# Linear-attention numerators: two feature groups in two 64-column halves of TensorE, in plain fp32 instead of split fp32r

## The chip, the cores and the metric

The kernel runs on one core of a Trainium2 chip. A core has a matrix engine (TensorE, PE in the profile; its weight loads are PEld), a vector engine (VectorE, DVE), an engine for functions and copies (ScalarE, ACT), a general one (GpSimd, POOL) and one that here only issues transfers (SyncE, SP). The metric is device time in microseconds (us), lower is better. Three runs of the kernel before took 760.90, 761.03 and 761.24 us; the median is 761.03.

## The reference

For 2048 rows x of 640 features, the output is a gated sum g * a + (1 - g) * b, with g the sigmoid of a row's product with a vector. b is a feed-forward block (640 to 1728 with SiLU, and back). a is linear attention with 32 heads of 20 features; the changed part lies in its last lines:

```
phi_q = concatenate([softmax(pq), softmax(-pq)])        # 40 features a head
kv  = einsum("bhsf,bhsd->bhfd", phi_k, v)               # 40 x 20 a head
num = einsum("bhqf,bhfd->bhqd", phi_q, kv)              # the numerators
den = einsum("bhqf,bhf->bhq", phi_q, z) + 1e-6
a   = (num / den) @ wo
```

The kernel divides by the denominators, and multiplies by g, in the features of q before the numerators are formed, so that the numerators go straight on to the product with wo.

## The kernel before, in words

TensorE multiplies a stationary operand (at most 128 rows by 128 columns, loaded as weights) with a moving one. The kernel reaches fp32 accuracy with the reduced type fp32r by splitting each operand into a high part and the remainder: the high part is a copy by ACT, the remainder a subtraction by DVE or POOL (`split`), and a product is three matmuls, high by high, high by low and low by high (`PASSES`). Three places use plain fp32 matmuls instead: the products of small weights (lines 231 and 317) and the transposes with an identity (lines 898, 946 and 991).

The work goes in stages: keys and values and their sums per head (the last of their projections, L470, starts at 172 us), the feed-forward block in four blocks of 512 rows (L518 and L706), and then the queries, in 8 pieces of 256 rows. In the last stage the projections of later pieces (L429), their softmax features (on DVE, ACT and POOL) and the transposes, numerators and output products of earlier pieces take turns.

For one piece u the steps are these:

- `t_mm(u, i)` transposes the features with PE (L991). The 32 heads have 1280 feature columns. They are taken in groups of 120 columns, three heads each; a pair i (0 to 4) holds two such groups, and i = 5 holds the last 80 columns, two heads. The result, up to 120 partitions by 2 x 256, is in PSUM.
- `t_hi` copies it to SBUF as the high part (ACT, L1002), `t_lo` makes the low part (DVE, L1008).
- `n_mm(u, gp, a)` forms the numerators of pair i = 2 gp + a: 120 features by 256 rows against `kvw`, whose blocks are 120 columns wide. The first group of a pair fills the first 60 columns of its block and zeros stand in the other 60; the second group the other way about. So the six matmuls of a pair (two groups, three passes) add up in the same 120 partitions of PSUM (L1128). The rest has three matmuls.
- `n_hi`, `n_lo` split the numerators into high and low (L1142, L1144, L1150) for the next product.
- `w_mm` multiplies them with `wo` (L1171), with 120 partitions a pair, and the result is added to the feed-forward part and stored.

`make_kvw` (L886) prepares `kvw` and `kvwr` (for the rest) once: transposes of the sums per head, a split into high and low, zeros by POOL. `wo_load` and `wo_split` bring in `wo` in five chunks of 120 rows.

The order is written out by hand. Inside the last stage `inorder(PE, DVE, ACT, POOL)` fixes the order of each of these engines to that of the code in `step(u)` for u = 1 to 5 and `last_steps` after them; all loads and stores are on SP's queue. A middle step contains, on PE, the numerators of pairs 4 and 5 of the piece before, then for piece u pairs 0, 1, 2 and 3, each followed by other work, with projections and output products between.

Of the kernel before, what the change touches and what calls it, by code (L numbers as in the profile page):

```python
# [16 lines left out]
P = 128  # L17
S = 2048
D = 640
# [9 lines left out]
FR = F - NF * P  # L29
GR = 6  # L30
GW = GR * DH
NG = H // GR
REST = D - NG * GW
NJ = 2 * NG + 1
# [26 lines left out]
def mix_kernel(ctx: ExitStack, tc: tile.TileContext, xT, wqT, wkc, wkr, wv, bd, bdc, cst, wo, w1, w1r, w2, out):  # L61
# [665 lines left out]

    def wo_load(c):
        wor_raw[c] = r = raw(f"wo{c}")
        nc.sync.dma_start(r[:GW, :D], wo[c * GW : (c + 1) * GW, :])  # L730

    def wo_split(c):
        r = wor_raw.pop(c)
        split(WO[:GW, c, 0, :D], WO[:GW, c, 1, :D], r[:GW, :D])

    def stack(dst, src, hi, col, n=GW):

# [148 lines left out]

    def make_kvw():

        parts = [w.rearrange("p j f -> p (j f)").rearrange("p (i q f) -> p i q f", q=4, f=KD) for w in kvw]
# [12 lines left out]
        for j0, n, pt in pts:  # L902
            n = min(n, 2 * NG - j0)
            i0, i1 = j0 // 2, (j0 + n) // 2
# [12 lines left out]

    es = {}

# [72 lines left out]
                    pT[:w, jj * 256 + k * P : jj * 256 + (k + 1) * P], es[2 * PB[u] + k][:, j * GW : j * GW + w], ident  # L992
                )

    def t_hi(u, i):
        pT = fTs[u, i]
        nj, w = (2, GW) if i < NG else (1, RC)
        if (u, i) < (0, 4):
            f = slot(f"fT{u}_{i}")
        else:  # L1000
            f = slot(f"fT{u}_{i}", fu, "u", 3) if i % 2 == 0 else slot(f"fT{u}_{i}", tb, "fT", 2)
        nc.scalar.copy(f[:w, 0, : nj * 256], pT[:w, : nj * 256])  # L1002
        fTs[u, i] = f, pT

    def t_lo(u, i):
        f, pT = fTs[u, i]
        nj, w = (2, GW) if i < NG else (1, RC)
        nc.vector.tensor_tensor(  # L1008
            f[:w, 1, : nj * 256], pT[:w, : nj * 256], f[:w, 0, : nj * 256].bitcast(F32), op=ALU.subtract
        )  # L1010
        fTs[u, i] = f

    for n in range(2):
# [2 lines left out]
    with inorder(PE, DVE, ACT, POOL):  # L1016
        last_dense(2)
        last_dense(3)
        load_gates(NB - 1)
        load_fused(0)  # L1020
        last_dense(4)
        WQ = big("wq")
        zbc = wslot("zbc")
        nc.sync.dma_start(zbc, kv_d[KF].partition_broadcast(P))

        def fuse(gi):
            return fused(kvb["bd"], WQ[:, :, 0, :], WQ[:, :, 1, :], gi)
# [23 lines left out]
        kvw = [wslot(f"kvw{h}", F32R)[:GW, : 2 * NG * GW].rearrange("p (j f) -> p j f", f=GW) for h in range(2)]  # L1051
        kvwr = fu.tile([RC, 2, GW], F32R, name="kvwr")
# [36 lines left out]
        acc_mm(1)  # L1089
        acc_out(1)  # L1090
        acc_mm(2)
        acc_out(2)
        for i in range(4):
            t_mm(0, i, bank)
            t_hi(0, i)
            t_lo(0, i)
# [15 lines left out]
    WOR = tb.tile([GW, D], F32R, name="wor_s")  # L1112
    wor = raw("wor")
    for k in range(3):
        nc.sync.dma_start(wor[k * REST : (k + 1) * REST, :D], wo[NG * GW :, :])

    def n_mm(u, gp, a):
        if (gp, a) == (0, 0):
            oTs[u] = tb.tile([GW, 2, NG + 1, 256], F32R, tag="oT", name=f"oT{u}", bufs=2)
        if a == 0:  # L1120
            pns[u, gp] = single(f"pn{u}_{gp}").rearrange("p (a s) -> p a s", a=2)
        i = 2 * gp + a
        nj, w = (2, GW) if i < NG else (1, RC)
        f = fTs.pop((u, i))
        n = 0
        for jj in range(nj):
            for hk, hp in PASSES:
                nc.tensor.matmul(  # L1128
                    pns[u, gp][:GW, a, :],
                    kvw_of(hk, 2 * i + jj)[:w],  # L1130
                    f[:w, hp, jj * 256 : (jj + 1) * 256],
                    start=(n == 0),
                    stop=(n == 3 * nj - 1),
                )
                n += 1

    pns = {}

    def n_hi(u, gp):
        o, pn = oTs[u], pns[u, gp]  # L1140
        if gp < 2:
            nc.scalar.copy(o[:, 0, 2 * gp : 2 * gp + 2, :], pn[:GW])  # L1142
        else:
            nc.scalar.copy(o[:, 0, 4, :], pn[:GW, 0])  # L1144
            nc.scalar.activation(o[:, 1, 5, :], pn[:GW, 1], AF.Copy, scale=stk[:GW, 0:1])

    def n_lo(u, gp):
        o, pn = oTs[u], pns.pop((u, gp))
        k = slice(2 * gp, 2 * gp + 2) if gp < 2 else slice(4, 5)
        nc.vector.tensor_tensor(o[:, 1, k, :], pn[:GW, : k.stop - k.start], o[:, 0, k, :].bitcast(F32), op=ALU.subtract)  # L1150
        if gp == 2:
            nc.vector.scalar_tensor_tensor(
                o[:, 0, 5, :], pn[:GW, 1], stk[:GW, 1:2], o[:, 1, 5, :].bitcast(F32), op0=ALU.mult, op1=ALU.add
            )

    ws = {}
# [1 line left out]
    def w_mm(u, m0, n):  # L1158
# [9 lines left out]
        for a in range(n):  # L1168
            ds = slice((m0 + a) * P, (m0 + a + 1) * P)
            for k, (c, ho, hw) in enumerate(todo):  # L1170
                nc.tensor.matmul(  # L1171
                    pa[:, a, :],
                    WO[:GW, c, hw, ds] if c < NG else WOR[:, ds],
                    o[:, ho, c, :],
                    start=(k == 0),
                    stop=(k == len(todo) - 1),
                )
# [49 lines left out]
    def t_pair(u, i):  # L1227
        for k in (i, i + 1):
            t_mm(u, k)
        for k in (i, i + 1):  # L1230
            t_hi(u, k)

    def n_first(u):
        n_mm(u, 0, 0)
        t_mm(u, 2)
        t_hi(u, 2)
        n_mm(u, 0, 1)
        t_mm(u, 3)
        n_hi(u, 0)
        t_hi(u, 3)  # L1240

    def n_second(u):
        n_mm(u, 1, 0)
# [2 lines left out]
        n_mm(u, 1, 1)  # L1246

    def second_out(u):
        t_hi(u, 4)
        t_hi(u, 5)  # L1250
        n_hi(u, 1)
        t_lo(u, 4)
        t_lo(u, 5)
        n_lo(u, 1)

    def step(u):
# [3 lines left out]
        n_lo(u - 1, 2)  # L1260
        if u == 1:
            on(a, lambda t: q_sub(t, 1), q_exp)
        t_lo(u, 0)
        t_lo(u, 1)
        if u == 1:
            on(a, q_norm, q_sum)
            x_next(2)
# [2 lines left out]
        if u > 1:  # L1270
            on(a, q_small)
        n_first(u)
        t_lo(u, 2)
        if u > 1:
            on(b, q_max)
        n_lo(u, 0)
        t_lo(u, 3)
        if u == 1:
            on(a, q_small)
            on(b, q_max)  # L1280
# [29 lines left out]
    def last_steps(u):  # L1310
# [4 lines left out]
        t_pair(u, 0)  # L1315
        on(a, q_norm_sum)
        on(b, q_max)
        t_lo(u, 0)
        on(b, lambda t: q_sub(t, 0))
        t_lo(u, 1)  # L1320
        w_mm(u - 1, 0, 2)
        on(b, lambda t: q_sub(t, 1))
        w_out(u - 1, 0)
# [8 lines left out]
            t_mm(u, i)  # L1332
        n_hi(u, 0)
        for i in (2, 3):
            t_hi(u, i)
        t_lo(u, 2)
        n_lo(u, 0)
        t_lo(u, 3)
        on(b, q_norm_sum, q_small, q_mul)
        w_mm(u - 1, 2, 2)  # L1340
        n_second(u)
# [5 lines left out]
            for i in range(2):  # L1347
                t_mm(v, i, ks=(k,))
        w_copy(u - 1, 4)
        t_hi(v, 0)  # L1350
        n_mm(u, 2, 0)
        n_mm(u, 2, 1)
        t_lo(v, 0)
        t_hi(v, 1)
        t_lo(v, 1)
        w_add(u - 1, 4)
        n_hi(u, 2)
        n_lo(u, 2)
        n_first(v)
        t_lo(v, 2)  # L1360
        n_lo(v, 0)
        t_lo(v, 3)
        w_mm(u, 0, 2)
        n_second(v)
        w_out(u, 0)
# [11 lines left out]
    with inorder(PE, DVE, ACT, POOL):  # L1377
# [4 lines left out]
            n_lo(0, gp)  # L1382
        for i in (4, 5):
            t_mm(0, i)
            t_hi(0, i)
            t_lo(0, i)
# [72 lines left out]
```

## Time and profile before

| | before |
|---|---|
| median of 3 runs | 761.03 us |
| span of the profiled execution | 759.8 us |
| PE busy | 755.0 us |
| DVE busy | 371.6 us |
| ACT busy | 266.4 us |
| POOL busy | 264.3 us |
| first and last start of the numerators' matmuls | 578.6 and 744.9 us |

The profiled execution's own time is known by its span, from its first to its last instruction. A group row of the profile gives line, engine and operation, then what is written and read, the shape, the count, the busy time in us and the mean length of one in ns. For a matmul, 120*120 120x256 means a stationary operand of 120 rows and 120 columns and a moving one of 120 rows and 256 columns. The length of one matmul includes its way through the array, which overlaps with the next matmul, so the price of one in a run of equal ones is the distance of their starts. A row of the timeline gives the start in us, the length in us and how many like instructions in a row it stands for. Times in square brackets, or after the second bar, are idle time of the engine before the instruction and what ended it.

### The profile page before, as it was taken

The numbers are of one execution on the slowest core, as the hardware profiler recorded it, in microseconds if no ns is written. First come the engines' busy times: TensorE is split into PE (matmuls) and PEld (weight loads), VectorE is DVE, ScalarE is ACT, GpSimd is POOL, SyncE is SP. The second block draws the span as 40 slices with busy tenths as digits, with TensorE's granted clock in tenths as the row PEclk, the third lists the DMA queues.
The fourth block names the chain that finished last, engine by engine and source line by source line (L and its number), as shares of the span: only waits on it lengthen the run. The fifth ranks groups of instructions, "written<-read, shape, count | busy, mean of one in ns | idle before, by whom it ended". The sixth has DMA issues, their size and how long they took to land.

```text
span 759.8 us, 10642 instructions
## 1 busy us (share of the span) xinstructions
PE 755.0 (99%) x4249; PEld 664.9 (88%) x4249; DVE 371.6 (49%) x664; ACT 266.4 (35%) x483; POOL 264.3 (35%) x165
## 2 busy tenths in 40 slices
PE   9999999999999999999999999999999999999998
PEld 8888888888888888888888888888999999999998
DVE  4676666676641221112211122134578888787861
ACT  5444444337541311122111222224354443334341
POOL 2388777768000000000000000000356766855551
PEclk9999999999999999999999999999999999999999
DMA  7111111112650220002200014022003332111222
GB/s 254 54 53 53 53 53 53 60 49 83 206 175 1 69 83 1 1 0 72 84 0 1 1 40 154 8 81 85 6 29 127 97 104 70 54 52 43 70 70 91
DMA packets 35259, 50.17 MB, mean 66 GB/s; under 512 B 3541, under 2 KB 22885, under 8 KB 35210
## 3 DMA queue, kind: packets, MB, share of 16 engines
q1 hardware_dynamic: 35210, 49.50, 20.7%
q8 instruction: 33, 0.54, 0.3%
q14 instruction: 16, 0.13, 0.1%
HBM read 38.37 MB, written 11.11 MB: 65 GB/s over the span
## 4 chain that ended last, share of the span: by engine, by line
PE 97%; DVE 1%; DMA 0%; POOL 0%; ACT 0%; issue 0%; SPq 0%; POOLq 0%; DVEq 0%; ACTq 0%
PE acc L706 25%; PE ph L518 23%; PE kvp L470 16%; PE pq L429 9%; PE pa L1171 9%; PE pn L1128 4%; PE kv L440 2%; PE pT L991 2%; PE kvp L535 2%; PE kvp L328 1%; PE kvq L328 1%; PE pwk L317 1%; PE pwq L231 1%; DMA wvr<-wv 0%; POOL eq L840 0%; PE kvp L451 0%
## 5 line engine op out<-in xcount | busy, mean ns | idle before, releaser
L120 DVE TENSOR_TENSOR u<-ph,u 128x512 fp32r<-128x512 f32 x48 | 33.2, 692 | 188.5 <-ACT u L118 188.5
L706 PE MATMUL acc<-u,w 128*128 128x512 f32 x480 | 114.2, 391 | 0.0
L891 POOL MEMSET kvw<- 120x600 f32 x2 | 1.2, 598 | 321.1 <-PE ph L518 321.1
L706 PEld LDWEIGHTS acc<-u,w 128*128 128x128 f32 x480 | 89.7, 188 | 19.2
L518 PE MATMUL ph<-xf,w 128*128 128x512 f32 x420 | 99.7, 390 | 0.0
L521 ACT ACTIVATE ph<-ph 128x512 f32<-128x512 f32 x48 | 27.9, 582 | 192.6 <-PE ph L518 192.6
L518 PEld LDWEIGHTS ph<-xf,w 128*128 128x128 f32 x420 | 78.7, 188 | 16.6
L470 PE MATMUL kvp<-wh,xa 128*128 128x500 f32 (+1 forms) x420 | 93.0, 357 | 0.0
L470 PEld LDWEIGHTS kvp<-wh,xa 128*128 128x128 f32 x420 | 71.4, 188 | 9.9
L1171 PE MATMUL pa<-oT,wo 120*128 120x256 f32 x600 | 76.8, 282 | 0.0
L1171 PEld LDWEIGHTS pa<-oT,wo 120*128 120x128 f32 x600 | 73.7, 188 | 0.0
L706 PE MATMUL acc<-u,f 128*128 128x512 f32 x300 | 73.0, 394 | 0.0
L518 PE MATMUL ph<-xf,f 128*128 128x512 f32 x300 | 72.7, 394 | 0.0
L518 PEld LDWEIGHTS ph<-xf,f 128*128 128x128 f32 x300 | 56.4, 188 | 13.1
L706 PEld LDWEIGHTS acc<-u,f 128*128 128x128 f32 x300 | 56.1, 188 | 12.8
L804 POOL TENSOR_TENSOR ez<-eq,zbc 128x1280 f32<-128x1280 f32 x16 | 48.1, 3005 | 41.3 <-ACT eq L787 41.2
L120 POOL TENSOR_TENSOR ph<-ek,ph 128x1280 fp32r<-128x1280 f32 x16 | 47.4, 2964 | 26.8 <-ACT ph L118 26.8
L429 PE MATMUL pq<-wq,xb 128*128 128x320 f32 x360 | 55.5, 311 | 0.0
L429 PEld LDWEIGHTS pq<-wq,xb 128*128 128x128 f32 x360 | 53.0, 188 | 0.0
L470 PE MATMUL kvp<-wl,xa 128*128 128x500 f32 (+1 forms) x210 | 47.4, 356 | 0.0
L840 POOL TENSOR_TENSOR eq<-eq,sm 128x1280 f32<-128x1280 f32 x16 | 37.9, 2368 | 15.1 <-DVE sm L834 13.9
L498 POOL TENSOR_TENSOR ek<-ek,st 128x1280 f32<-128x1280 f32 x16 | 38.0, 2376 | 9.2 <-issue 6.1
(161 smaller groups left out, 1121.8 us busy)
## 6 DMA issues: line engine op xcount, KB each, us to landing
wr<-w SPq DMA_DIRECT2D x26, 320.0 KB, 3.9
xrf<-xT SPq DMA_DIRECT2D x20, 256.0 KB, 3.8
fb_d<-o SPq DMA_DIRECT2D x20, 256.0 KB, 2.4
y<-fb_d SPq DMA_DIRECT2D x16, 256.0 KB, 2.9
out<-y SPq DMA_DIRECT2D x16, 256.0 KB, 2.1
xra<-xT SPq DMA_DIRECT2D x14, 256.0 KB, 3.1
xrb<-xT SPq DMA_DIRECT2D x12, 256.0 KB, 2.7
wvr<-wv SPq DMA_DIRECT2D x5, 321.0 KB, 5.2
```

Source lines behind the costliest of these rows:

```text
L120: eng.tensor_tensor(lo, src, hi.bitcast(F32), op=ALU.subtract)
L328: nc.tensor.matmul(kv_cols(t, lo, hi), x_of(t)[c][:, hx, :], WKV[hw][:, c, lo:hi], start=(opens and hx == 0 and hw == 0), stop=(c == NC - ...
L429: nc.tensor.matmul(dst, xt[c][:, hx, :], w[:, c, hw, lo : lo + n], start=first, stop=(hx == 1 and c == NC - 1))
L470: nc.tensor.matmul(kv_cols(t, lo, hi), xt[c][:, hx, :], WKV[hw][:, c, lo:hi], start=(n == 0), stop=(n == 3 * NC - 1), skip_group_check=True,)
L498: nc.gpsimd.tensor_tensor(groups(e), groups(e), spread(st[:, 1, :]), op=ALU.mult)
L518: nc.tensor.matmul(ph, lhs, rhs, start=(n == 0), stop=(n == len(todo) - 1))
L521: nc.scalar.activation(hs, ph, AF.Silu)
L706: nc.tensor.matmul(acc[m], lhs, rhs, start=(f == order[0] and n == 0), stop=(f == order[-1] and n == len(todo) - 1))
L804: nc.gpsimd.tensor_tensor(ez, Q[t]["e"], zbc, op=ALU.mult)
L840: nc.gpsimd.tensor_tensor(groups(q["e"]), groups(q["e"]), spread(q["sm"][:, 2 * H : 4 * H]), op=ALU.mult)
L1128: nc.tensor.matmul(pns[u, gp][:GW, a, :], kvw_of(hk, 2 * i + jj)[:w], f[:w, hp, jj * 256 : (jj + 1) * 256], start=(n == 0), stop=(n == 3 * ...
L1171: nc.tensor.matmul(pa[:, a, :], WO[:GW, c, hw, ds] if c < NG else WOR[:, ds], o[:, ho, c, :], start=(k == 0), stop=(k == len(todo) - 1),)
```

## The change

The matmuls of the numerators are in plain fp32, and the two groups of a pair no longer add up in the same 120 columns. Each group gets a half of the array: the first writes partitions 0 to 63 of PSUM, the second 64 to 127, and each block of `kvw` is 64 columns wide (60 in use, 4 zero). A pair is two matmuls, one a side, each starting and ending its own sum. The rest is likewise two matmuls, of 64 and of 56 columns.

With no split of the operands, `t_hi` becomes `t_out`, one copy by ACT to fp32, and `t_lo` is gone with its places in the order. `make_kvw` copies by ACT once, and POOL clears only the four spare columns. The numerators now lie on 128 partitions, so `wo` is handed over with four rows of zeros after each 60 of its first 600 rows, and is loaded, split and used in chunks of 128 rows. The numbers of output matmuls, of loads and of stores, and the order of all other work, stay.

```diff
+CT = P // 2
...
-        nc.sync.dma_start(r[:GW, :D], wo[c * GW : (c + 1) * GW, :])
+        nc.sync.dma_start(r[:, :D], wo[c * P : (c + 1) * P, :])
...
-        split(WO[:GW, c, 0, :D], WO[:GW, c, 1, :D], r[:GW, :D])
+        split(WO[:, c, 0, :D], WO[:, c, 1, :D], r[:, :D])
...
-        for h in range(2):
-            nc.gpsimd.memset(parts[h][:, :, 1:3].bitcast(F32), 0.0)
+        nc.gpsimd.memset(kvw[:, :, KD:], 0.0)
...
-            split(
-                *(part[:, i0:i1, ::3] for part in parts),
-                pt[:GW, : n * KD].rearrange("p (i a f) -> p i a f", a=2, f=KD),
-            )
-        split(
-            *(kvwr[:, h].rearrange("p (k f) -> p k f", f=REST) for h in range(2)),
+            nc.scalar.copy(kvw[:, j0 : j0 + n, :KD], pt[:GW, : n * KD].rearrange("p (j f) -> p j f", f=KD))
+        nc.scalar.copy(
+            kvwr.rearrange("p (k f) -> p k f", f=REST),
             pt[:RC, None, n * KD : n * KD + REST].to_broadcast([RC, KH, REST]),
         )
...
-    def kvw_of(h, j):
-        return kvw[h][:, j, :] if j < 2 * NG else kvwr[:, h, :]
+    def kvw_of(i, side):
+        if i < NG:
+            return kvw[:, 2 * i + side, :]
+        return kvwr[:, :CT] if side == 0 else kvwr[:, CT:]
...
-    def t_hi(u, i):
+    def t_out(u, i):
...
-        nc.scalar.copy(f[:w, 0, : nj * 256], pT[:w, : nj * 256])
-        fTs[u, i] = f, pT
-
-    def t_lo(u, i):
-        f, pT = fTs[u, i]
-        nj, w = (2, GW) if i < NG else (1, RC)
-        nc.vector.tensor_tensor(
-            f[:w, 1, : nj * 256], pT[:w, : nj * 256], f[:w, 0, : nj * 256].bitcast(F32), op=ALU.subtract
-        )
+        f = f[:, 0, :].bitcast(F32)
+        nc.scalar.copy(f[:w, : nj * 256], pT[:w, : nj * 256])
         fTs[u, i] = f
...
-            oTs[u] = tb.tile([GW, 2, NG + 1, 256], F32R, tag="oT", name=f"oT{u}", bufs=2)
+            oTs[u] = tb.tile([P, 2, NG + 1, 256], F32R, tag="oT", name=f"oT{u}", bufs=2)
...
-        n = 0
-        for jj in range(nj):
-            for hk, hp in PASSES:
-                nc.tensor.matmul(
-                    pns[u, gp][:GW, a, :],
-                    kvw_of(hk, 2 * i + jj)[:w],
-                    f[:w, hp, jj * 256 : (jj + 1) * 256],
-                    start=(n == 0),
-                    stop=(n == 3 * nj - 1),
-                )
-                n += 1
+        w = GW if i < NG else RC
+        for side in range(2):
+            lhs = kvw_of(i, side)
+            k = side if i < NG else 0
+            nc.tensor.matmul(
+                pns[u, gp][side * CT : side * CT + lhs.shape[-1], a, :],
+                lhs,
+                f[:w, k * 256 : (k + 1) * 256],
+                start=True,
+                stop=True,
+            )
...
-                    WO[:GW, c, hw, ds] if c < NG else WOR[:, ds],
-                    o[:, ho, c, :],
+                    WO[:, c, hw, ds] if c < NG else WOR[:, ds],
+                    o[:, ho, c, :] if c < NG else o[:GW, ho, c, :],
...
-        "wo": wo,
+        "wo": np.concatenate([rows(wo[: NG * GW].reshape(2 * NG, KD, D), CT).reshape(NG * P, D), wo[NG * GW :]]),
```

More of the change, by code (lines that the diff above doesn't have):

```diff
@@ L887, in make_kvw @@
     def make_kvw():
-        parts = [w.rearrange("p j f -> p (j f)").rearrange("p (i q f) -> p i q f", q=4, f=KD) for w in kvw]
-        for h in range(2):
-            nc.gpsimd.memset(parts[h][:, :, 1:3].bitcast(F32), 0.0)
+        nc.gpsimd.memset(kvw[:, :, KD:], 0.0)
         pts = []
@@ L1050, in mix_kernel @@
         wo_load(4)
-        kvw = [wslot(f"kvw{h}", F32R)[:GW, : 2 * NG * GW].rearrange("p (j f) -> p j f", f=GW) for h in range(2)]
-        kvwr = fu.tile([RC, 2, GW], F32R, name="kvwr")
+        kvw = wslot("kvw")[:GW, : 2 * NG * CT].rearrange("p (j f) -> p j f", f=CT)
+        kvwr = fu.tile([RC, GW], F32, name="kvwr")
         w = make_kvw()
@@ L1094, in mix_kernel @@
             t_mm(0, i, bank)
-            t_hi(0, i)
-            t_lo(0, i)
+            t_out(0, i)
         acc_mm(3)
@@ L1114, in mix_kernel @@
     for k in range(3):
-        nc.sync.dma_start(wor[k * REST : (k + 1) * REST, :D], wo[NG * GW :, :])
+        nc.sync.dma_start(wor[k * REST : (k + 1) * REST, :D], wo[NG * P :, :])
     def n_mm(u, gp, a):
         if (gp, a) == (0, 0):
-            oTs[u] = tb.tile([GW, 2, NG + 1, 256], F32R, tag="oT", name=f"oT{u}", bufs=2)
+            oTs[u] = tb.tile([P, 2, NG + 1, 256], F32R, tag="oT", name=f"oT{u}", bufs=2)
         if a == 0:
@@ L1122, in n_mm @@
         i = 2 * gp + a
-        nj, w = (2, GW) if i < NG else (1, RC)
         f = fTs.pop((u, i))
-        n = 0
-        for jj in range(nj):
-            for hk, hp in PASSES:
-                nc.tensor.matmul(
-                    pns[u, gp][:GW, a, :],
-                    kvw_of(hk, 2 * i + jj)[:w],
-                    f[:w, hp, jj * 256 : (jj + 1) * 256],
-                    start=(n == 0),
-                    stop=(n == 3 * nj - 1),
-                )
-                n += 1
+        w = GW if i < NG else RC
[9 more added lines that the diff above has]
+            )
     pns = {}
@@ L1141, in n_hi @@
         if gp < 2:
-            nc.scalar.copy(o[:, 0, 2 * gp : 2 * gp + 2, :], pn[:GW])
+            nc.scalar.copy(o[:, 0, 2 * gp : 2 * gp + 2, :], pn)
         else:
-            nc.scalar.copy(o[:, 0, 4, :], pn[:GW, 0])
-            nc.scalar.activation(o[:, 1, 5, :], pn[:GW, 1], AF.Copy, scale=stk[:GW, 0:1])
+            nc.scalar.copy(o[:, 0, 4, :], pn[:, 0])
+            nc.scalar.activation(o[:GW, 1, 5, :], pn[:GW, 1], AF.Copy, scale=stk[:GW, 0:1])
     def n_lo(u, gp):
@@ L1149, in n_lo @@
         k = slice(2 * gp, 2 * gp + 2) if gp < 2 else slice(4, 5)
-        nc.vector.tensor_tensor(o[:, 1, k, :], pn[:GW, : k.stop - k.start], o[:, 0, k, :].bitcast(F32), op=ALU.subtract)
+        nc.vector.tensor_tensor(o[:, 1, k, :], pn[:, : k.stop - k.start], o[:, 0, k, :].bitcast(F32), op=ALU.subtract)
         if gp == 2:
             nc.vector.scalar_tensor_tensor(
-                o[:, 0, 5, :], pn[:GW, 1], stk[:GW, 1:2], o[:, 1, 5, :].bitcast(F32), op0=ALU.mult, op1=ALU.add
+                o[:GW, 0, 5, :], pn[:GW, 1], stk[:GW, 1:2], o[:GW, 1, 5, :].bitcast(F32), op0=ALU.mult, op1=ALU.add
             )
@@ L1230, in t_pair @@
         for k in (i, i + 1):
-            t_hi(u, k)
+            t_out(u, k)
     def n_first(u):
@@ L1235, in n_first @@
         t_mm(u, 2)
-        t_hi(u, 2)
+        t_out(u, 2)
         n_mm(u, 0, 1)
@@ L1239, in n_first @@
         n_hi(u, 0)
-        t_hi(u, 3)
+        t_out(u, 3)
     def n_second(u):
@@ L1248, in second_out @@
     def second_out(u):
-        t_hi(u, 4)
-        t_hi(u, 5)
+        t_out(u, 4)
+        t_out(u, 5)
         n_hi(u, 1)
-        t_lo(u, 4)
-        t_lo(u, 5)
         n_lo(u, 1)
@@ L1262, in step @@
             on(a, lambda t: q_sub(t, 1), q_exp)
-        t_lo(u, 0)
-        t_lo(u, 1)
         if u == 1:
@@ L1272, in step @@
         n_first(u)
-        t_lo(u, 2)
         if u > 1:
@@ L1276, in step @@
         n_lo(u, 0)
-        t_lo(u, 3)
         if u == 1:
@@ L1317, in last_steps @@
         on(b, q_max)
-        t_lo(u, 0)
         on(b, lambda t: q_sub(t, 0))
-        t_lo(u, 1)
         w_mm(u - 1, 0, 2)
@@ L1334, in last_steps @@
         for i in (2, 3):
-            t_hi(u, i)
-        t_lo(u, 2)
+            t_out(u, i)
         n_lo(u, 0)
-        t_lo(u, 3)
         on(b, q_norm_sum, q_small, q_mul)
@@ L1349, in last_steps @@
         w_copy(u - 1, 4)
-        t_hi(v, 0)
+        t_out(v, 0)
         n_mm(u, 2, 0)
         n_mm(u, 2, 1)
-        t_lo(v, 0)
-        t_hi(v, 1)
-        t_lo(v, 1)
+        t_out(v, 1)
         w_add(u - 1, 4)
@@ L1359, in last_steps @@
         n_first(v)
-        t_lo(v, 2)
         n_lo(v, 0)
-        t_lo(v, 3)
         w_mm(u, 0, 2)
@@ L1384, in mix_kernel @@
             t_mm(0, i)
-            t_hi(0, i)
-            t_lo(0, i)
+            t_out(0, i)
         on(0, q_mm)
```

1 line of the change is left out of this document (removed).

## The prediction

> **What bounds the kernel now.** I read the page from the top: the span and the busy time of each engine, the granted clock by slice, then the chain of work that ended last.
>
> ```profile
> span 759.8 us, 10642 instructions
> PE 755.0 (99%) x4249; PEld 664.9 (88%) x4249; DVE 371.6 (49%) x664; ACT 266.4 (35%) x483; POOL 264.3 (35%) x165
> PEclk9999999999999999999999999999999999999999
> PE 97%; DVE 1%; DMA 0%; POOL 0%; ACT 0%; issue 0%; SPq 0%; POOLq 0%; DVEq 0%; ACTq 0%
> PE acc L706 25%; PE ph L518 23%; PE kvp L470 16%; PE pq L429 9%; PE pa L1171 9%; PE pn L1128 4%; PE kv L440 2%; PE pT L991 2%; PE kvp L535 2%; PE kvp L328 1%; PE kvq L328 1%; PE pwk L317 1%; PE pwq L231 1%; DMA wvr<-wv 0%; POOL eq L840 0%; PE kvp L451 0%
> ```
>
> TensorE (PE) is busy for 99% of the span at the full clock and carries 97% of the chain; no other engine reaches half. The changed matmuls (L1128) are 4% of that chain. All of them lie after 578 us, so I asked for the busy time by stretches there.
>
> ```profile
> 640.00:680.00 40.00, 40.00 (x318) 40.00 (x317) 32.20 (x52) 15.21 (x28) 26.94 (x17) 1.00 0.16 50
> 680.00:720.00 40.00, 40.00 (x322) 39.99 (x321) 32.30 (x56) 12.68 (x23) 21.30 (x11) 1.00 0.22 67
> ```
>
> The columns are PE, weight load (PEld), DVE, ACT, POOL, clock, DMA share, GB/s. PE has no idle time: what lengthens its own list of work lengthens the kernel by as much, and what is taken from DVE or ACT gives nothing back unless PE waits for it. The sum is therefore one over PE time.
>
> **What is removed from PE.** The profile's timeline of PE gives start and length of each run of like matmuls. The first four rows are from a middle step, the next three hold the last feature group (80 features, three matmuls), the last is the opening run of 24.
>
> ```profile
> 642.07 0.87 PE L1128 MATMUL pn<-fT,kvw 120*120 120x256 f32 x6
> 642.77 0.60 PE L991 MATMUL pT<-ident,eq 128*120 128x128 f32 x4
> 643.13 0.95 PE L1128 MATMUL pn<-fT,kvw 120*120 120x256 f32 x6
> 643.92 0.60 PE L991 MATMUL pT<-ident,eq 128*120 128x128 f32 x4
> 586.50 0.86 PE L1128 MATMUL pn<-fT,kvw 120*120 120x256 f32 x6
> 587.21 0.51 PE L1128 MATMUL pn<-fT,kvwr 80*120 80x256 f32 x3
> 587.56 1.04 PE L991 MATMUL pT<-ident,eq 128*120 128x128 f32 x8
> 578.60 2.99 PE L1128 MATMUL pn<-fT,kvw 120*120 120x256 f32 x24
> ```
>
> Ends are modelled and overlap the next run, so price by starts: six matmuls take 642.77 - 642.07 = 0.70 us, three take 587.56 - 587.21 = 0.35 us, which is 0.117 us for each 256-column matmul. There are 8 pieces of 256 rows, each with five pairs of feature groups and the rest: 240 + 24 matmuls, as the counts below say. Removed: 40 x 0.70 + 8 x 0.35 = 30.8 us.
>
> ```profile
> L1128 PE MATMUL pn<-fT,kvw 120*120 120x256 f32 x240 | 35.4, 285 | 0.0
> L1128 PE MATMUL pn<-fT,kvwr 80*120 80x256 f32 x24 | 4.1, 280 | 0.0
> L231 PE MATMUL pwq<-constb,wTq 120*128 120x120 f32 x50 | 6.4, 274 | 0.0
> L231 PE MATMUL pwq<-constb,wTq 40*128 40x40 f32 x10 | 1.3, 281 | 0.0
> L991 PE MATMUL pT<-ident,eq 128*120 128x128 f32 x160 | 22.6, 273 | 0.2 <-POOL eq L840 0.2
> L518 PE MATMUL ph<-xf,w 128*128 128x512 f32 x420 | 99.7, 390 | 0.0
> ```
>
> **What is added to PE: passes.** For each of the 48 pairs there come two matmuls in plain fp32, one for each 64-column half. The two L231 rows show what plain fp32 is: line 231 issues 25 matmuls of 120 columns and 5 of 40, and the trace has 50 and 10. So a plain fp32 matmul is two passes, each with its weight load, and 48 pairs make 96 matmuls and 192 passes in place of 264.
>
> No row has such a pass with 256 moving columns. Its neighbours:
>
> ```profile
> 488.21 1.27 PE L231 MATMUL pwq<-constb,wTq 120*128 120x120 f32 x10
> 528.10 1.30 PE L231 MATMUL pwq<-constb,wTq 40*128 40x40 f32 x10
> 197.65 1.29 PE L518 MATMUL ph<-xf,w 128*128 128x512 f32 x5
> ```
>
> A run's length less that of its last matmul (the means above), over the steps between, is the price of one. Ten passes of 120 columns: (1.27 - 0.27) / 9 = 0.11 us each. Ten of 40 columns come out at the same 0.11, so these are bound by the weight load of 128 columns and bound the streaming only from above. The L991 transposes stream plain fp32 too: eight of 128 columns from 587.56 are (1.04 - 0.27) / 7 = 0.11 us apart, half the speed of the fp32r matmul, which does 256 columns in 0.117. Twice that for 256 columns is 0.22 us. Bounds: 0.117 (plain fp32 streams as fast as fp32r) and 0.23 (the 512-column fp32r matmul, (1.29 - 0.39) / 4). I take 0.22, the nearest in kind. A pair then has four passes, 0.88 us one after another, against 0.70 before; 0.44 if the halves overlap wholly.
>
> PE issues in order: half A pass 1, A pass 2, B pass 1, B pass 2. A pass 2 needs A's columns, so it waits for A pass 1; B pass 1 needs others and can start beside A pass 2. If halves overlap, a lone pair lasts three passes, 0.66 us, plus the part of B's weight load that is not hidden; 64 columns are half of the load that took 0.11, so 0.05: 0.71 us. A pair that follows at once adds two passes, 0.44, to 0.55 with both exposed loads: I take 0.50. The order of PE's instructions in the changed kernel has the 48 pairs in 35 separate runs, since transposes or other matmuls stand between: 25 lone pairs, 8 of two, one of three, one of four. So 25 x 0.71 + 8 x 1.21 + 1.71 + 2.21 = 31.4 us. Ends: 28.8 us with every load hidden (131 pass lengths of 0.22), 32.7 us with 0.73 and 0.55.
>
> Whether two column halves overlap, no row of this trace shows. Bounds are 0.44 and 0.88 a pair; I take the overlap in issue order, since B's first pass writes other columns and other partitions than A's second and has nothing of it to wait for. The Trainium skill ("TensorE: Matmul & The Clock Gate", Part 3) reports three column tiles running 2.38 times as fast as one after another, with about 4 ns between starts; no run here shows it. By that figure, with pairs started together, the passes would be an estimated 48 x 0.444 = 21.3 us in place of 31.4, and the sum 10.1 us lower.
>
> **What is added to PE: the change of tiling.** The array must go from one 128-column tile to halves and back, 35 times. The trace has no column halves, but it has matmuls on 40 rows, which use half the array's rows, between full ones. The 40-column run at 528.10 above is one; what stands around it on PE, then the weight loads, and a second place:
>
> ```profile
> 527.32 0.85 PE L518 MATMUL ph<-xf,w_r 128*128 128x512 f32 x3
> 529.34 0.97 PE L706 MATMUL acc<-u,w 128*128 128x512 f32 x3
> 527.55 0.19 PEld L518 LDWEIGHTS ph<-xf,w_r 128*128 128x128 f32 x1
> 528.10 1.19 PEld L231 LDWEIGHTS pwq<-constb,wTq 40*128 40x128 f32 x10 [0.36 <-DVE wo L120]
> 529.34 0.76 PEld L706 LDWEIGHTS acc<-u,w 128*128 128x128 f32 x4
> 20.37 1.27 PE L317 MATMUL pwk<-stage 120*128 120x120 f32 x10
> 21.57 0.41 PE L317 MATMUL pwk<-stage,stage 40*128 40x40 f32 x2
> 21.92 0.72 PE L328 MATMUL kvp<-wh,xa 128*128 128x500 f32 x2
> ```
>
> Normally a weight load runs under the matmul before it. Here the first load on each side of the 40-row run stands alone with its matmul. At 527.32: 3 x 0.23 + 10 x 0.112 would let L706 start at 529.13; its third matmul ends at 529.34 + 0.97 = 530.31, so started 0.39 before, at 529.92, and the first, two steps of 0.23 earlier, in effect at 529.46: 0.33 us lost for going in and out. At 20.37: 12 x 0.112 gives 21.71; the second L328 ends at 22.64 and started at 22.25, the first in effect 0.225 earlier at 22.02: 0.31 us lost. I take 0.32 a round trip, 35 x 0.32 = 11.2 us; bounds 0 (column halves do not count as such a change) and 0.33. The row tiles are the nearest thing, so the upper end. The Trainium skill ("TensorEngine Tiling (Array Packing)", Tiling Modes, Key Properties) says that changing the tiling mode drains TensorE while changing only the tile does not; the 0.31 and 0.33 agree for row tiles, and no run here shows it for columns.
>
> **Off PE.** DVE loses the split of the transposed features:
>
> ```profile
> L1008 DVE TENSOR_TENSOR fT<-pT,fT 120x512 fp32r<-120x512 f32 x39 | 26.0, 684 | 18.1 <-ACT fT L1002 18.1
> L1008 DVE TENSOR_TENSOR fT<-pT,fT 80x256 fp32r<-80x256 f32 x8 | 3.3, 411 | 0.0
> L120 DVE TENSOR_TENSOR u<-ph,u 128x512 fp32r<-128x512 f32 x48 | 33.2, 692 | 188.5 <-ACT u L118 188.5
> 729.50 0.60 PE L991 MATMUL pT<-ident,eq 128*120 128x128 f32 x4
> 730.26 0.65 PE L991 MATMUL pT<-ident,eq 128*120 128x128 f32 x4 [0.15 <-POOL eq L840]
> ```
>
> The 29 us of the two L1008 rows lay under PE, which did not idle, and give nothing. The numerators now wait for ACT's copy alone; the one gap of note in the last steps is 0.15 us, behind POOL, and stays. I put the gain at zero, at most 0.3 us. ACT's copy of the features stays, in as many instructions. The kvw split and one POOL memset go too, far ahead of their use. The five wo loads keep their places on SP's queue and grow from 120 to 128 rows of 640 fp32 (300 to 320 KB each). Copies on 128 rows in place of 120 cost the same, as 692 and 684 ns for 512 columns show. The output matmuls (L1171) keep count and columns. Nothing is moved past anything on any queue.
>
> **Sum.** 31.4 + 11.2 - 30.8 = +11.8 us on the profiled execution of 759.8 us: 771.6 us of span. The median of the runs is 761.03, 1.2 us more than that span, so the time is 772.8 us; 770.0 with all loads hidden and 774.5 with none and 0.33.
>
> **Rivals.**
> *Halves do not overlap* (the change does not do what it says). Each pair 0.88: 42.2 + 11.2 - 30.8 = +22.6, 783.7 us; with 0.229 a pass and 0.33 a switch 785.7. For it: nothing in the trace runs two matmuls at a time.
> *Going to halves and back is free.* 31.4 - 30.8 = +0.6, 761.6 us; 759.0 with loads hidden. For it: only row tiles show the loss. Against it: both kinds re-divide the array.
> *The halves start together*, PE taking B's first pass ahead of A's second. Two passes of 0.22 a pair: 21.1 + 11.2 - 30.8 = +1.5, 762.5 us. Against it: PE's matmuls in the trace are in program order throughout. This is where the 4 ns of the Trainium skill (same page and section) would lead; no run here shows it.
> *A plain fp32 pass streams 256 columns in 0.117 us*: a lone pair 0.40, a further one 0.25, together 17.3; 17.3 + 11.2 - 30.8 = -2.3, 758.7 us, faster. It decides from 131 passes p + 2.5 < 19.6, so p under 0.13. For it: the 0.11 of L231 is the weight load's. Against it: the transposes' 0.11 for 128 columns.
>
> **How the numbers follow.** Forecast 0.48 (slower), no overlap 0.21 (slower), free switch 0.15 (0.05 faster, 0.08 the same, 0.02 slower), start together 0.08 (0.04 the same, 0.04 slower), fast pass 0.06 (faster), both of the gains at once 0.02 (faster). That makes faster 0.13, the same 0.12, slower 0.75, where 0.2% (1.5 us) is what a measurement here can tell from no change. The range goes from 760, inside the free switch, to 786, past the end of no overlap; the forecast's own is 770 to 774.5.
>
> **What would show it.** In the changed profile: 192 passes on the numerators' line instead of 264; starts of A pass 2 and B pass 1 within 0.1 us of each other (overlap) or 0.22 apart (none); 0.22 between pass 1 and 2 of a half; the weight load after each run standing with its matmul, 0.1 us after the last pass ended (switch); DVE about 30 us less busy; and each middle step longer by 4 x 0.71 + 1.21 + 5 x 0.32 - 3.85 = 1.8 us. The chain of work in order of time gives a step's length now, 662.37 - 637.81 = 24.6 us between the same projection of two steps:
>
> ```profile
> 637.81 4.42 PE pq L429 x30
> 662.37 4.42 PE pq L429 x30
> ```
>
> The forecast is wrong if a pass takes well under 0.2 us, if loads are prefetched across the switch, or if PE idles in the last steps.

## The result and the profile after

The changed kernel took 763.77 us (median of 5 runs, 763.47 to 764.17), the kernel before 761.03 us beside it (760.81 to 761.38). The ratio is 1.0035, 95% interval 1.0024 to 1.0046: slower by 2.7 us, where 11.8 us were forecast. Its profiled execution has a span of 762.3 us, 2.5 us more than before.

First the page of the kernel after: the span, the busy time of each engine, and the chain of work that ended last, by engine.

```profile
span 762.3 us, 10460 instructions
PE 756.8 (99%) x4177; PEld 643.5 (84%) x4177; DVE 345.5 (45%) x613; ACT 268.0 (35%) x483; POOL 262.1 (34%) x164
PE 97%; POOL 1%; DMA 1%; DVE 0%; SPq 0%; ACT 0%; issue 0%; POOLq 0%; DVEq 0%; ACTq 0%
```

PE still bounds the kernel. DVE has 26 us less to do, and none of it shows in the span. Next the groups of instructions by shape, of the last stage. The numerators are on line 1117 now:

```profile
L1117 PE MATMUL pn<-fT,kvw 120*64 120x256 f32 x160 | 25.2, 401 | 0.0
L1117 PE MATMUL pn<-fT,kvwr 80*64 80x256 f32 x16 | 4.8, 379 | 0.0
L1117 PE MATMUL pn<-fT,kvwr 80*56 80x256 f32 x16 | 4.8, 379 | 0.0
```

160 + 16 + 16 = 192 passes, as worked out. The timeline of PE in a middle step and, as its last row, the opening run of four pairs; then the weight loads of the same middle step:

```profile
644.08 0.65 PE L1117 MATMUL pn<-fT,kvw 120*64 120x256 f32 x4
644.66 0.65 PE L988 MATMUL pT<-ident,eq 128*120 128x128 f32 x4
645.25 0.65 PE L1117 MATMUL pn<-fT,kvw 120*64 120x256 f32 x4
645.83 0.65 PE L988 MATMUL pT<-ident,eq 128*120 128x128 f32 x4
646.24 2.02 PE L1159 MATMUL pa<-oT,wo 128*128 128x256 f32 x15
...
580.90 1.95 PE L1117 MATMUL pn<-fT,kvw 120*64 120x256 f32 x16
```

```profile
644.08 0.20 PEld L1117 LDWEIGHTS pn<-fT,kvw 120*64 120x64 f32 x4 [0.20 <-issue]
644.66 0.41 PEld L988 LDWEIGHTS pT<-ident,eq 128*120 128x120 f32 x4 [0.39 <-issue]
```

Three readings.

- *The halves run together, and from the first pass on.* The opening run's 16 passes take 1.95 us, of which the last pass is 0.40. So 1.55 us lie between the first start and the last. As eight slots of two passes that is 1.55 / 7 = 0.22 us a slot. The records of its single passes say the same: the two passes of a slot start 6 to 7 ns apart, the slots 0.216 us, but for the first slot of each run, which lasts 0.267. A record does not name its half, but with the last 80 features it can be told by the columns: a pass with 64 starts at 613.301 us, one with 56 at 613.308. A lone pair is two slots, 0.43 us, where the prediction had 0.71; the 0.05 us more of the first slot are counted with the switch below.
- *The switch is there.* The lone pair's row starts 0.58 us before the transposes that follow it, 0.15 us more than its two slots. Transposes with output products behind them hold PE for 646.24 - 645.83 = 0.41 us; the same four with a pair behind them hold it for 645.25 - 644.66 = 0.59, 0.18 us more. That makes 0.33 us in and out. The weight loads stand idle for 0.20 and 0.39 us before, on "issue", which means that the profile shows nothing that they waited for.
- *The last stage explains little of the 2.5 us.* The chain in order of time has that stage's steps at the projections below, 24.8 us apart, against 24.6 before: 0.25 us a step, where 1.8 were forecast. That is some 1.2 us over the five steps of `step(u)`, but the runs of several pairs at the stage's start and end win most of it back (the opening four pairs take 4 x 0.43 + 0.3 = 2.0 us by these prices, in place of 2.8): from the first numerator to the end of the span are 181.4 us, against 181.2 before.

```profile
614.93 4.41 PE pq L430 x30
639.74 4.41 PE pq L430 x30
664.55 4.41 PE pq L430 x30
689.37 4.41 PE pq L430 x30
```

The first numerator starts at 580.90 us, against 578.60 before. So 2.3 of the 2.5 us are lost before it. The chain in order of time, at the start and near the end of the feed-forward block (L706 before, L707 after), first of the kernel before, then of the kernel after:

```profile
188.74 6.80 PE acc L706 x30
566.70 6.18 PE acc L706 x27
```

```profile
188.90 6.80 PE acc L707 x30
568.74 6.29 PE acc L707 x27
```

From one to the other are 377.96 us before and 379.84 after: 1.9 us more over work that the diff does not touch. The busy time by stretches of 200 to 560 us shows PE without idle time in both, and with 9 matmuls fewer in the same 360 us (before, then after):

```profile
200.00:560.00 360.00, 360.00 (x1638) 297.79 (x1638) 94.79 (x152) 97.57 (x169) 14.17 (x13) 1.00 0.17 52
```

```profile
200.00:560.00 360.00, 360.00 (x1629) 296.01 (x1628) 92.11 (x145) 97.69 (x169) 11.30 (x11) 1.00 0.17 52
```

The groups by shape of that stretch (before, then after) say which matmuls got longer:

```profile
L706 PE MATMUL acc<-u,w 128*128 128x512 f32 x401 | 95.5, 391 | 0.0
L518 PE MATMUL ph<-xf,w 128*128 128x512 f32 x396 | 94.1, 390 | 0.0
L706 PE MATMUL acc<-u,f 128*128 128x512 f32 x300 | 73.0, 394 | 0.0
L518 PE MATMUL ph<-xf,w_r 128*128 128x512 f32 x40 | 9.9, 394 | 0.0
```

```profile
L707 PE MATMUL acc<-u,w 128*128 128x512 f32 x402 | 96.6, 393 | 0.0
L519 PE MATMUL ph<-xf,w 128*128 128x512 f32 x390 | 93.2, 392 | 0.0
L707 PE MATMUL acc<-u,f 128*128 128x512 f32 x300 | 73.0, 394 | 0.0
L519 PE MATMUL ph<-xf,w_r 128*128 128x512 f32 x40 | 10.1, 397 | 0.0
```

Those with the weights w and w_r are 2 to 3 ns longer each, those with f are not. From start to start it is the same: the mean goes from 229.1 to 231.4 ns for acc<-u,w, and is 232.4 in both for acc<-u,f. Order, shapes and clock are alike and the other engines nearly so, so I compared the addresses in the built kernels. `kvwr`, the block for the last 80 columns, held 2 x 120 numbers a partition (960 bytes) and holds 120 now (480). Tiles of later pools moved down by 480 bytes, the feed-forward weights w1_10 to w1_12, w2_9 to w2_12 and both w_r among them; f, the other weights and the moving operands stayed. The rows above mix the two kinds of w: the weights that moved went from 229.0 to 233.3 ns a step, those that stayed kept their 227.

### The profile page after: what moved, and what is told of

It is laid out like the page before. It is cut to its first block, busy times and chain, and to the rows that moved or that the text cites. A ratio compares the mean times of both kernels' runs of the same rounds, so it can differ in the third digit from the quotient of the medians.

```text
span 762.3 us, 10460 instructions
## 1 busy us (share of the span) xinstructions
PE 756.8 (99%) x4177; PEld 643.5 (84%) x4177; DVE 345.5 (45%) x613; ACT 268.0 (35%) x483; POOL 262.1 (34%) x164
## 3 DMA queue, kind: packets, MB, share of 16 engines
q1 hardware_dynamic: 35255, 49.60, 20.7%
## 4 chain that ended last, share of the span: by engine, by line
PE 97%; POOL 1%; DMA 1%; DVE 0%; SPq 0%; ACT 0%; issue 0%; POOLq 0%; DVEq 0%; ACTq 0%
PE acc L707 25%; PE ph L519 23%; PE kvp L471 16%; PE pq L430 9%; PE pa L1159 9%; PE pn L1117 3%; PE pT L988 3%; PE kv L441 2%; PE kvp L536 2%; PE kvp L329 1%; PE kvq L329 1%; PE pwq L232 1%; PE pwk L318 1%; DMA wvr<-wv 1%; POOL ez L805 0%; POOL eq L841 0%
## 5 line engine op out<-in xcount | busy, mean ns | idle before, releaser
L707 PE MATMUL acc<-u,w 128*128 128x512 f32 x480 | 115.2, 393 | 0.0
L707 PEld LDWEIGHTS acc<-u,w 128*128 128x128 f32 x480 | 89.6, 188 | 20.3
L1159 PE MATMUL pa<-oT,wo 128*128 128x256 f32 x600 | 77.3, 282 | 0.0
L1159 PEld LDWEIGHTS pa<-oT,wo 128*128 128x128 f32 x600 | 73.6, 188 | 1.2 <-ACT fT L1000 0.8
L707 PE MATMUL acc<-u,f 128*128 128x512 f32 x300 | 73.0, 394 | 0.0
L707 PEld LDWEIGHTS acc<-u,f 128*128 128x128 f32 x300 | 56.1, 188 | 12.9
```

The costliest lines, as they stand in the source:

```text
L707: nc.tensor.matmul(acc[m], lhs, rhs, start=(f == order[0] and n == 0), stop=(f == order[-1] and n == len(todo) - 1))
L1159: nc.tensor.matmul(pa[:, a, :], WO[:, c, hw, ds] if c < NG else WOR[:, ds], o[:, ho, c, :] if c < NG else o[:GW, ho, c, :], start=(k == 0) ...
```

## The experiments

Three theories stood at the start: the passes of the two halves start in pairs; the switch costs 0.3 us a run of pairs; the feed-forward block is slower for the address of its weights.

### The addresses: the changed kernel with the old ones, the old kernel with new ones

```diff
-        kvwr = fu.tile([RC, GW], F32, name="kvwr")
+        kvwr = fu.tile([RC, 2 * GW], F32, name="kvwr")[:, :GW]
```

> The changed kernel with the tile kvwr given its old 960 bytes again (the second half unused), so that every tile behind it lies where it lay before the change, in the feed-forward stage above all. Theory: the change itself costs PE about +0.3 us, and 2.2 us of the measured 2.7 come from the feed-forward weights that moved by 480 bytes, off a multiple of 64: 761.0 to 761.8 us, PE at 577 us of the trace within 0.3 us of the kernel before, and the matmuls acc<-u,w back from a mean step of 231.5 ns to 229.3. Rival (the numerators' change itself, or something else of it, costs all): 763.8 us and a shift of 2 us at 577 us as before.

Measured: 761.37 us (11 runs), ratio 1.0003 (0.9994 to 1.0012). With the old addresses the changed kernel takes the time of the kernel before.

The other way about, the kernel before with eight numbers (32 bytes) more behind `kvwr`, and with sixteen (64 bytes):

```diff
-        kvwr = fu.tile([RC, 2, GW], F32R, name="kvwr")
+        kvwr = fu.tile([RC, 2 * GW + 8], F32R, name="kvwr")[:, : 2 * GW].rearrange("p (h f) -> p h f", h=2)
```

> The kernel before with 32 bytes more behind kvwr and nothing else, so that the weights of the last feed-forward tiles start 32 bytes off a multiple of 64. Theory: about 500 matmuls become 4 ns slower, 2.0 us, 763.0 us. Rival (address plays no part): 761.0 us.

> The kernel before with 64 bytes more behind kvwr: as much is moved as with 32, but the weights stay on multiples of 64. Theory: 761.0 us, as before. Rival (any move of the tiles costs): 763 us.

Measured: 763.18 us with 32 bytes, ratio 1.0028 (1.0017 to 1.0039); 760.49 us with 64, ratio 0.9992 (0.9983 to 1.0000). The same two rows of the chain, of the changed kernel with the old addresses and then of the old kernel with 32 bytes more:

```profile
188.27 6.80 PE acc L707 x30
566.23 6.18 PE acc L707 x27
```

```profile
188.01 6.80 PE acc L706 x30
567.85 6.29 PE acc L706 x27
```

377.96 and 379.84 us: each kernel has the other's block when it has the other's addresses. So 2.4 of the 2.7 us are not the numerators' at all, and a pad of 32 bytes does the same to the old kernel. The 64 bytes were a little better than none, which was not expected; it comes back below.

### Plain fp32 over the full width

The numerators in plain fp32 as one 120-column tile, as before: no halves, no switch, `wo` unpadded, and `kvwr` at its old size. Of the difference from the changed kernel only the matmul itself is shown.

```diff
-        for side in range(2):
-            lhs = kvw_of(i, side)
-            k = side if i < NG else 0
+        for jj in range(nj):
             nc.tensor.matmul(
-                pns[u, gp][side * CT : side * CT + lhs.shape[-1], a, :],
+                pns[u, gp][:GW, a, :],
...
-                start=True,
-                stop=True,
+                start=(jj == 0),
+                stop=(jj == nj - 1),
```

> Plain fp32 alone, without halves: the kernel before with its blocks of 120 columns and zeros, one plain fp32 matmul for each group in place of three passes, the transposed features copied once and not split, wo as before, addresses as before. Theory (halves run side by side, a pass of 256 columns takes 0.216 us, the switch of tiling costs 0.3 us): four passes a pair one after another, 48 x 0.864 = 41.5 us in place of 30.8 and no switch, 771.7 us. Rival (the pair's 0.43 us in the changed kernel comes from cheap fp32 passes of 0.11 us, not from overlap): 48 x 0.44 = 21 us, 751 us.

Measured: 767.61 us, ratio 1.0090 (1.0076 to 1.0104). The expectation was 4 us too high by a miscount: the last 80 columns need one matmul at full width, not two. With 40 x 4 + 8 x 2 = 176 passes of 0.216 us, 38.0 - 30.8 = +7.2 us would have been 768.2. Its timeline of PE:

```profile
644.43 1.03 PE L1120 MATMUL pn<-fT,kvw 120*120 120x256 f32 x4
645.29 0.60 PE L989 MATMUL pT<-ident,eq 128*120 128x128 f32 x4
645.73 1.03 PE L1120 MATMUL pn<-fT,kvw 120*120 120x256 f32 x4
```

Four passes take 645.29 - 644.43 = 0.86 us, 0.215 each: the forecast's 0.22 for a pass was right. The four transposes behind them take 0.44 with a full-width matmul next, in place of the 0.59 of the kernel after, though the matmul that follows waits for the same copy by ACT in both; so that wait hardly explains the 0.18 us. Against this kernel the two halves are worth 767.61 - 761.37 = 6.2 us, switches included.

### Fewer switches

The changed kernel with the old addresses, and in each step pairs 0 and 1, and pairs 2 and 3, issued together: 22 runs of pairs instead of 35.

```diff
+        n_mm(u, 0, 1)
...
-        n_mm(u, 0, 1)
...
+        n_mm(u, 1, 1)
...
-        n_mm(u, 1, 1)
```

> The changed kernel at the old addresses, with the numerators of pairs 0 and 1, and of 2 and 3, issued together, ahead of the transposes that stood between them: 22 runs of numerators in place of 35, all else the same. Theory (going to halves and back costs 0.30 us a run, a pair 0.43 wherever it stands): 13 x 0.30 = 3.9 us less than the 761.4 of the same without it, 757.5 us. Rival (the switch is nearly free and the cost lies in the passes): no change, 761.4 us. If PE then waits for ACT's copies of the features, less is won and PE shows idle time before the numerators.

Measured: 757.87 us, ratio 0.9958 (0.9946 to 0.9971). 761.37 - 757.87 = 3.5 us for 13 runs is 0.27 us a switch. The timeline of PE at the same place:

```profile
640.32 1.08 PE L1117 MATMUL pn<-fT,kvw 120*64 120x256 f32 x8
641.33 1.09 PE L988 MATMUL pT<-ident,eq 128*120 128x128 f32 x8
642.17 2.00 PE L1159 MATMUL pa<-oT,wo 128*128 128x256 f32 x15
```

Two pairs take 1.01 us, against 0.58 for a lone one: a further pair costs its two slots of 0.22 and nothing else. Two pairs and their eight transposes take 642.17 - 640.32 = 1.85 us, where the kernel after needs 646.24 - 644.08 = 2.16.

### How far ahead PE looks

On top of this, the four matmuls of two pairs in the order left, left, right, right, in place of left, right, left, right.

```diff
+        if a == 0:
+            return
+        for side, i in ((0, 2 * gp), (0, 2 * gp + 1), (1, 2 * gp), (1, 2 * gp + 1)):
```

> Pairs together as in the run of 757.9 us, but the four matmuls of two pairs are issued half by half: first half of pair one, first half of pair two, second half of pair one, second half of pair two. Theory (PE takes matmuls of a free half ahead of those that wait for the other, from further back than the next one): the halves still run side by side, 757.9 us, two starts 7 ns apart from the first pass on. Rival (PE reaches only to the next matmul, or issues in strict order): seven pass lengths in place of four for two pairs, 24 times 0.65 us more, 773 us, with single starts at the head of each run.

Measured: 757.96 us, ratio 0.9957 (0.9943 to 0.9971), against 757.87 us and 0.9958 in the other order. Its timeline of PE:

```profile
640.30 1.09 PE L1119 MATMUL pn<-fT,kvw 120*64 120x256 f32 x8
641.33 1.09 PE L988 MATMUL pT<-ident,eq 128*120 128x128 f32 x8
```

Eight passes again take 1.03 us. In the records of the single passes they start in twos, 13 to 14 ns apart, from the first slot on. Where the second pair is the rest, the records tell the halves apart. The order of issue there is pair 4 left, the rest left (64 columns), pair 4 right, the rest right (56 columns). All four passes of pair 4 start first, at 609.676, 609.690, 609.943 and 609.956 us, and only then the rest's, at 610.159 with 64 columns and 610.172 with 56. So the right half of pair 4 ran ahead of the left matmul that stood before it. With one half's passes one behind the other, the right half's first pass starts beside the left half's first, ahead of three left passes that stand before it in PE's queue. So two column halves are served as two queues here, and the halves' order in the code did not matter, at least over two pairs.

### What the address has to be

The 64 bytes above had helped, so I supposed that weights want to start at a multiple of 64 bytes. The large tiles of weights have rows of 642 numbers, 2568 bytes, which start at all sorts of addresses. With rows of 640, and the tile a little longer so that all blocks start at multiples of 64:

```diff
-        return wp.tile([P, 2, NC, D + 2], F32R, tag="big", name=name, bufs=2)
+        return wp.tile([P, NC * WC + 54], F32R, tag="big", name=name, bufs=2)
...
-        return big_tile(name).rearrange("p s c d -> p c s d")
+        return big_tile(name)[:, : 2 * NC * D].rearrange("p (s c d) -> p c s d", s=2, c=NC)
```

This was put into the changed kernel with the old addresses, the kernel before, and the kernel with pairs together.

> The changed kernel at the old addresses but with the two large tiles that hold ten of the feed-forward weights, and later the weights of q and wo, laid out with rows of 640 columns in place of 642, so that every weight block in them starts on a multiple of 64 bytes. Theory (a weight block off a multiple of 64 bytes costs about 4 ns a matmul of 512 columns): some 520 matmuls of the feed-forward block gain 4 ns, 2.1 us, and the output matmuls 0 to 3 ns each, 0 to 1.8 us: 757.5 to 759.3 us. Rival (what helped was the old place of the tiles, not the multiple of 64): 761.4 us or more.

> The kernel before with the same rows of 640 columns in the two large tiles. Theory: the same gain on the numerators as they were, 2.1 to 3.9 us, 757.1 to 759.0 us. Rival: 761.1 us or more.

> Both: pairs together and the large tiles on multiples of 64 bytes, in the changed kernel at the old addresses. Theory: the gains add, 3.9 + 2.1 to 3.9 us off 761.4: 753.6 to 755.4 us, faster than both kernels of this study.

Measured: 761.60 us (ratio 1.0008, 0.9999 to 1.0017), 761.94 us (1.0013, 1.0004 to 1.0022) and 758.35 us (0.9966, 0.9953 to 0.9978). Nothing was gained, in three places: the theory fell.

Sorting the steps from start to start of the 512-column matmuls of all these runs by the addresses in the built kernels gave another order: not the address of the weights counted, but its distance from that of the moving operand, modulo 256 bytes (or 512; both fitted so far). Before the change the weights that moved stood at 128 modulo 256 and the moving operands at 192; after it these weights stood at 160. With 64 bytes more they stood at 192, like the moving operands. In the aligned kernels the moving operands had moved to 0, and the large tiles had come to lie 128 off. The same weights at 192 took 229.0 ns a step there, where they took 227.2 with the moving operands at 192 too (the kernel with 64 bytes more), so their own address does not decide. So I put all weights and moving operands of the feed-forward block at the same offset modulo 256, on top of the pairs together, and with the rows of 640 numbers of the aligned kernels:

```diff
-        return wp.tile([P, D + 2], F32, tag="raw", name=name, bufs=4)
+        return wp.tile([P, D + 16], F32, tag="raw", name=name, bufs=4)[:, : D + 2]
...
-        return wp.tile([P, 2, NC, D + 2], F32R, tag="big", name=name, bufs=2)
+        return wp.tile([P, 6464], F32R, tag="big", name=name, bufs=2)
...
-        kvwr = fu.tile([RC, 2 * GW], F32, name="kvwr")[:, :GW]
+        kvwr = fu.tile([RC, 192], F32, name="kvwr")[:, :GW]
```

> Pairs together as in the run of 757.9 us, and all tiles laid out so that the feed-forward weights (the large tiles with rows of 640 columns too) and the moving tiles start at the same offset within 256 bytes; within 512 bytes one of the two large tiles and the last feed-forward weights lie 256 off. Theory A (a matmul is fast, 227 ns, when weights and moving operand have the same offset within 256 bytes): 600 matmuls with weights in the large tiles gain 4.5 ns, the 500 of the last feed-forward weights 2: 754.2 us. Theory B (the same offset within 512 bytes is needed): only the matmuls of one large tile gain, 756.5 us, and the two large tiles differ in the trace. Rival (offset plays no part beyond what the 32 and 64 bytes showed): 757.9 us.

Measured: 754.81 us, ratio 0.9916 (0.9902 to 0.9929), near the 754.2 of the theory of 256 bytes. This is the fastest kernel of the study: 6.5 us below the kernel before beside it (761.28), of which 757.87 - 754.81 = 3.1 us come from the offsets. Its groups by shape, its stretch of 200 to 560 us, and the two rows of its chain:

```profile
L707 PE MATMUL acc<-u,f 128*128 128x512 f32 x300 | 71.6, 390 | 0.0
L519 PE MATMUL ph<-xf,f 128*128 128x512 f32 x300 | 71.3, 389 | 0.0
```

```profile
200.00:560.00 360.00, 360.00 (x1661) 301.22 (x1660) 96.06 (x152) 100.44 (x171) 16.80 (x14) 1.00 0.17 53
```

```profile
188.58 6.80 PE acc L707 x30
562.54 6.15 PE acc L707 x27
```

The rows with f, which are the large tiles, fall from 394 to 390 and 389 ns. Weights 256 bytes off modulo 512 are as fast in this trace as those with none, 226.7 to 227.1 ns a step, which rules out the theory of 512 bytes. The stretch holds 23 matmuls more than before, and the block takes 373.96 us where it took 377.96. That is 4.0 us gained; the last stage gave 0.8 of them back (178.5 us from the first numerator to the end, against 177.7 in the kernel with pairs together), and no run says why.

## Why the prediction was wrong in size, and right in sign by luck

- **PE bounds, and only PE's list counts**: right. DVE lost 26 us and POOL a memset, with no gain, as put. PE stayed busy through the feed-forward block, and among the numerators the rows show it losing time at the switches alone.
- **192 passes of 0.22 us**: right; 0.215 at full width, 0.216 a slot in halves behind the first.
- **"If halves overlap, a lone pair lasts three passes"**: this is the step that failed. It let the right half's first pass start beside the left half's second, since PE issues in order. It starts 6 to 7 ns behind the left half's first, and 13 to 14 where it stands one matmul further back in the queue. A lone pair is 0.43 us and not 0.71, a further one 0.43 and not 0.50: 48 x 0.432 = 20.7 us in place of 31.4. That is 10.7 us of the sum. It was a rival ("the halves start together", chance 0.08). What was held against it, that PE's matmuls stand in program order throughout, came from rows in which no second half was free, so they could not speak on it. The Trainium skill ("TensorE: Matmul & The Clock Gate", Part 3) led to this rival with its starts some 4 ns apart, and the 6 to 7 ns here agree in kind. The same section says that matmuls start in strict program order; in the run half by half a matmul of the right half starts ahead of a left one queued before it, so the measurement decides.
- **Change of tiling, 35 x 0.32 us**: right. 0.27 us a run by the kernel with fewer switches, 0.33 by the rows of the middle step. The row tiles of the trace of before were a good guide to column halves, although the row at 528.10 us also carries a wait for DVE that the prediction did not set apart; the one at 20.37, without it, gave 0.31. The loss fits the Trainium skill ("TensorEngine Tiling (Array Packing)", Tiling Modes, Key Properties), by which a change of mode drains TensorE; the traces show the 0.27 to 0.33 us, not the drain itself.
- **30.8 us removed**: not measured by itself. The full-width kernel, with no switch in it, gives 38.0 - 6.5 = 31.5 us. The sum closes with 30.8: 20.7 + 35 x 0.30 - 30.8 = +0.4 us (-0.6 with 0.27 a switch, +1.5 with 0.33), and the changed kernel with the old addresses measured 761.37 against 761.08, +0.3, which is within the noise.
- **"Nothing is moved past anything on any queue"**: true of queues, and it let me miss what was moved, the addresses. `kvwr` at half its size put the later tiles 480 bytes lower, and some five hundred matmuls of the feed-forward block, at about 4 ns each, cost 2.1 us between that block's start and the first numerator, nearly all of the loss. This term was missing from the sum, put at nothing without a look at the addresses.
- **Range**: 763.8 lies within 760 to 786, but not within the forecast's own 770 to 774.5. The two errors, -10.7 and +2.1, are nearly the whole distance from 772.8.
- **Slower**: this came true by luck. With the old addresses the change takes the time of the kernel before (ratio 1.0003, 0.9994 to 1.0012); what made it slower was the term that the sum did not have.

## What to carry to other kernels

Two matmuls that are half as wide paid here when they came in long runs: each run of column halves cost some 0.3 us to enter and leave, so gather the pairs before splitting the array. When an edit changes a tile's size, look which addresses move behind it, and compare the time of stages that the edit does not touch before putting the difference down to the edit. In a matmul-bound kernel, try the same offset modulo 256 bytes in SBUF for weights and moving operands; it was worth 3.1 us here, more than the 2.4 us that the moved addresses had cost.

## What the runs showed of the hardware that was not expected

Two column halves of TensorE take work as two queues: the passes of one half ran beside those of the other, 6 to 14 ns apart, though up to three passes of the first stood before them in program order (757.96 and 757.87 us in the two orders). The section of the Trainium skill on tiling named above also says that different tiles can load and multiply in parallel, and this agrees: a pair takes 0.43 us, where its four passes take 0.86 at full width.

A matmul of 512 columns has a step that depends on the addresses of its two operands in SBUF, as far as these runs go by their distance modulo 256 bytes. With none it was 227 ns from start to start in most groups (means of 226.7 to 228.8), with 64 bytes 229 to 230, with 32 bytes 233.3 and with 128 bytes 232.5. The large tiles with mixed distances lay between: most of their blocks took 229 to 233 ns, but one, whose weights stood 40 bytes past the moving operand, took 227.5, so the same offset is not the only fast one. Few distances were looked at, in this kernel's order of reads, so this is a table of what was seen and not a law. That agreement modulo 256 makes the matmuls fast predicted one run (754.2 forecast, 754.81 measured) where modulo 512 gave 756.5. What in the chip makes it so stays open. The halves in split fp32r, which would use the 0.117 us matmul in place of the 0.216 us pass, were not tried.
